# The end of a backward chain: the last block's turned keys in another buffer, and four of its stores at the end of the order

## The chip, the cores and the metric

The kernel runs on one core of one Trainium2 chip. The metric is the device time of one execution in microseconds. The kernel before takes 2858.67 us, the median of three runs (2856.47 to 2862.91).

## The reference, cut to what matters

The forward pass is a sum of three terms: the input, a recurrent attention over segments of 32 rows with 8 memory rows that each segment hands to the next, and a two-layer feed-forward branch with a squared ReLU. The reference returns its output and the gradients of all ten inputs and weights.

```python
for s in range(n_seg):                      # 64 segments
    xs = x[:, s * seg_len:(s + 1) * seg_len, :].copy()
    h = jnp.concatenate([mem, xs], axis=1)  # 8 memory rows + 32 rows
    q = jnp.einsum('btd,dhe->bhte', h, Wq)  # k, v in the same way
    ...
    o = jnp.einsum('bhte,hed->btd', o, Wo)
    mem = o[:, :M, :].copy()
...
return x + _A_ref(xn, ...) + _B_ref(xn, ...)
...
_out, _vjp = jax.vjp(_f, A_x, A_mem0, A_Wq, A_Wk, A_Wv, A_Wo, B_w1, B_b1, B_w2, B_b2)
```

Because each segment's memory rows come from the segment before, the backward pass must go through the 64 segments one after the other, from the last to the first. The gradients of the four attention weights are products over all 2048 rows and all 512 memory rows ("left" rows in the code), and can be made once the chain is through.

## The kernel before, in words

The kernel has five stages: the feed-forward branch, the forward chain over 64 segments, a pass over the left rows, the backward chain over 64 segments, and the products that give the weight gradients. The change concerns the end of the backward chain and the beginning of the products.

*The backward chain.* Four segments make a block; there are 16 blocks, taken from block 15 down to block 0, so that "the last block" is block 0. A block has 128 ordinary rows and 32 left rows. The order of work is written by hand: `B_ORDER` (line 1158) is four strings of operation names, one for each segment of a block, and `play` (line 652) goes through them and calls the operations. Each `+` behind a name lets it run one place earlier: for a segment's operation one segment, for a block's operation (`L.` ahead of the name) one block. An operation that a block does not have under that name is skipped. On each queue the chain's instructions keep this order; loads of the next stage can stand between them.

The operations of block 0 that matter here, in the order in which `play` calls them, with the operations of the last segment in between:

- `vo0`, `vo1`, `ko0`, `qo0`, `ko1`, `qo1` (`so`, line 1245) store the block's value, key and query gradients from the tiles `gv`, `gk`, `gq` (`G4`, line 1191) to `S_GB` in DRAM, 512 KB each, on SP's queue. In the other blocks they are called `Vo0`, `Ko0` and so on and stand at other places of the strings.
- `qst` of block 1, called between `qo0` and `ko1` of block 0: the store of block 1's turned left queries from the buffer `gNat` to `S_GL`.
- `G`, `H`, `I` with a number (line 1260): products of the left rows with the weights on TensorE, into PSUM tiles `ps_RL`, summed by VectorE (line 1267).
- `ktr`, `vtr`, `qtr` (`nt`, line 1278): the left keys, values and queries are turned. For all blocks but block 0 a DMA transpose does it. For block 0 it is done by eight TensorE transposes into two PSUM tiles `ps_tr`, copied to SBUF by ScalarE and VectorE (lines 419 and 422).
- `kst`, `vst`, `qst` (line 1292): the turned rows are stored to `S_GL` on SP's queue.
- `gs` (line 1233): four transposes of the gradient rows into `ps_gm` and a copy; `sx` stores `S_XG`, `sl` stores `S_XGL`.

The turned rows of blocks 15 to 1 all lie in one buffer with the tag `gNat`, one after the other. Block 0's keys take the same buffer; its values and queries take the buffers of `gON` and `gOT`, which the last segment no longer needs. The tile `qN` (line 1343) holds the query rows of a segment for the backward products `kp0` and `kp1` (line 623); it is in the pool `be` and has one buffer. `ps_RL`, `ps_tr`, `ps_gm` and the chain's other single PSUM tiles share four banks, which go round.

*The products* (line 1506 on). Sixteen products come one after the other, each with 20 steps of accumulation over row groups `rc`, in the order 1 to 19 and then 0. The first takes its columns from `S_ON` and `S_OL` (tile `gn`) and its rows from `S_GM` and the gradient (tiles `GOc`). It works on eight output tiles in eight PSUM banks at once, so that each step has eight matmuls (line 1653). The second has the same rows and other columns, with four output tiles at a time. The key and query gradients in `S_GB` are read by the last eight products.

The tiles of this stage lie where those of the chain were; each load waits until the old tiles under it are free. Loads of the first three products are issued on GpSimd's queue in this order: quarters of `gn` alternating with groups of `GOc` (row groups 1 to 3, 4 to 7, 8 to 11, 12 to 15), four loads of the last group of `GOc`, four of `gn`'s left rows from `S_OL`, and then the second product's, of which one quarter goes on SP's queue. The group 0 of `GOc` goes on ScalarE's queue.

Of the kernel before, what the change touches and what calls it, by code (L numbers as in the profile page):

```python
# [10 lines left out]
BF16 = mybir.dt.bfloat16  # L11
F32 = mybir.dt.float32
P = 128
# [13 lines left out]
def kernel(  # L27
# [35 lines left out]
    L = M + SEG  # L63
# [39 lines left out]
    KH = H // HG  # L103
# [61 lines left out]
    def transpose_to(ps_ap, in_ap, base=0):  # L165
        k = in_ap.shape[0]
        nc.tensor.transpose(ps_ap, in_ap, ident[base:base + k, base:base + k])
# [42 lines left out]
    with sb("p1b", 2) as p1b, sb("p1", 1) as p1:  # L210
# [90 lines left out]
        for rb in range(NRB):  # L301
# [38 lines left out]
            xb = xq[rb]  # L340
# [77 lines left out]
    def acp(out, in_):  # L418
        nc.scalar.copy(out, in_)  # L419
# [15 lines left out]
    def turned_heads(W):  # L435

        return lambda h: W[:, :, h * P:(h + 1) * P]
# [263 lines left out]
    with psum("fr", 4) as fr, psum("fpp", 1) as fpp, \  # L701
# [5 lines left out]
        def tr(name):  # L707
            return fr.tile([P, 4 * P], BF16, name=name, tag="r")
# [11 lines left out]
        def block(b):  # L720

            if b not in blk:
                shapes = {"kL": (fs, [P, KH, HG, NL], BF16), "OT": (fs, [P, HG, KH, SPB, SEG], BF16),
                          "X": (fs, [P, DC, P], BF16),
                          "kM": (fo, [P, KH, HG, NL], BF16), "vTM": (fo, [P, KH, HG, NL], BF16),
                          "XT": (fs, [P, DC, SPB, SEG], F32), "qL": (fo, [P, KH, HG, NL], BF16),
                          "VL": (fs, [P, GW], BF16), "vM": (fo, [P, GW], BF16), "EL": (fo, [P, KH, KW], BF16),
                          "OTL": (fo, [P, KH, HG, NL], BF16),
                          "bb": (fo, [P, D], BF16)}

                def make(n):
                    if n == "X" and b == 0:
                        return X0
                    pool, shape, dt = shapes[n]
                    return pool.tile(shape, dt, name=n, tag=n)
                blk[b] = Tiles(make)
            return blk[b]
# [256 lines left out]
    with sb("la", 2) as la, sb("ls", 2) as ls, sb("lo", 1) as lo_, sb("wg", 2) as wg, psum("lpp", 1) as lpp, psum("lr", 4) as lr:  # L994
# [148 lines left out]
        with tc.manual_schedule():  # L1143
# [4 lines left out]
            for b in range(NB + 1):  # L1148
                for nm in LB_ORDER:
                    k = nm.rstrip("-")  # L1150
# [18 lines left out]
        "kg1+++++ qg1+++++ ra+++++ klb1+++++ L.H3+ ta+++++ rb+++++ tb+++++ Ha+++++ Hb+++++ xb+++++ o0mm++++++ L.ra3+ "  # L1169
# [20 lines left out]
    with sb("bq", 1) as bq, sb("bt", 1) as bt, sb("bs", 2) as bs, sb("be", 1) as be, psum("bpp", 1) as bpp, psum("br", 4) as br:  # L1190
# [30 lines left out]
        def left(b):  # L1221
            B_ = block(b)
            ps, st, o = {}, {}, {}
            src = {"v": "gvL", "k": "gkL", "q": "gqL"}
            o["lq"] = lambda: dma(B_["gqL"][:], S_GQL[b])

            def following(f):

                return lambda: f(b - 1) if b > 0 else None
            for n, f in loads.items():  # L1230
                o[n] = following(f)

            def gs():
                if b > 0:
                    nc.sync.dma_start_transpose(B_["GN"][:], gts[b][:].rearrange("p c r -> p (c r)"))
                else:
                    ps["gm"] = tr("ps_gm")
                    for c in range(DC):
                        transpose_to(ps["gm"][:, c * P:(c + 1) * P], gts[b][:, c, :])
                    acp(B_["GN"][:], ps["gm"][:].rearrange("p (c d) -> p c d", c=DC))  # L1240
            o["gs"] = gs
            o["gst"] = lambda: (dma if b > 0 else nc.scalar.dma_start)(S_GM[b], B_["GN"][:].rearrange("p c d -> p (c d)"))
            for t, n in enumerate("qkv"):
                for x in range(2):
                    def so(n=n, t=t, gs=slice(2 * x, 2 * x + 2) if n == "v" else slice(0, HG),
                           ks=slice(0, KH) if n == "v" else HALF[x]):
                        dma(S_GB[b, t][:, gs, ks], G4[n][:, gs, ks].rearrange("p g k j r -> p g k (j r)"))
                    o["%so%d" % (n.upper() if b > 0 else n, x)] = so

            jobs = [(turned_heads(Wqkv[t]), src[n], k) for t, n in ((2, "v"), (1, "k"), (0, "q")) for k in range(KH)]  # L1250
            for i in range(4):
                for x, nm in enumerate("GHI"):
                    def G_(i=i, x=x):
                        if ("R", i) not in ps:
                            ps["R", i] = big("ps_RL")
                            ps["n", i] = 0
                        ps["n", i] += 1
                        for m, (W, n, k) in enumerate(jobs[6 * i + 2 * x:6 * i + 2 * x + 2]):
                            for g in range(HG):
                                nc.tensor.matmul(ps["R", i][32 * g:32 * g + 32, :].rearrange("p (a b) -> p a b", b=P),  # L1260
                                                 lhsT=B_[n][:, k, g, :], rhs=W(g * KH + k), start=(ps["n", i] == 1 and m == 0),
                                                 stop=(ps["n", i] == 3 and m == 1), tile_position=(0, 32 * g))
                    o["%s%d" % (nm, i)] = G_
                if i == 0:
                    o["ra0"] = lambda: ENGS["L.ra0"](B_["R4"][:], ps["R", 0][:])
                else:
                    o["ra%d" % i] = lambda i=i: nc.vector.tensor_tensor(out=B_["R4"][:], in0=ps["R", i][:],
                                                                        in1=B_["R4"][:], op=ALU.add)
            turn_ops(o, big, lambda: B_["R4"], st)

            def xt():
                st["XL"] = bt.tile([P, DC, SPB, M], F32, name="b_XL", tag="XL" if b > 0 else "gST0")
                left_sums(st["XL"], st["T"])
            o["xt"] = xt
            o["sl"] = lambda: dma(S_XGL[b], st["XL"][:])

            for t, n in enumerate("qkv"):
                def nt(n=n):

                    tag = "gNat" if b > 0 else {"k": "gNat", "v": "gON", "q": "gOT"}[n]  # L1280
                    st[n] = bt.tile([P, KH, P], BF16, name="gNat", tag=tag)
                    if b > 0:
                        nc.sync.dma_start_transpose(st[n][:], B_[src[n]][:].rearrange("p k g r -> p k (g r)"))
                    else:
                        for p in range(2):
                            pt = tr("ps_tr")
                            for k in range(4):
                                transpose_to(pt[:, k * P:(k + 1) * P],
                                             B_[src[n]][:, 4 * p + k].rearrange("p g r -> p (g r)"))
                            (acp, vcp)[p](st[n][:, HALF[p], :], pt[:].rearrange("p (k e) -> p k e", k=4))  # L1290
                o[n + "tr"] = nt
                o[n + "st"] = lambda n=n, t=t: dma(S_GL[b].rearrange("g r t c -> (g r) t c")[:, t, :],
                                                   st[n][:].rearrange("p k e -> p (k e)"))

            o["sx"] = lambda: dma(S_XG[b], B_["XT"][:].rearrange("p c j r -> p c (j r)"))
            return o
# [209 lines left out]
    with sb("p5a", 1) as p5a, sb("p5h", 1) as p5h, sb("p5", 2) as p5, sb("p5g", 1) as p5g, \  # L1506
# [120 lines left out]
        for i, (t, g) in enumerate(COLS):  # L1627
# [16 lines left out]
            for x, js in enumerate(jobs[k:k + each] for k in range(0, len(jobs), each)):  # L1644
                if x in ((), (), (2, 6), (2, 6))[i] if i < 4 else x == 4:
                    b = todo.pop(0)
# [48 lines left out]
```

## Time and profile before

| | us |
|---|---|
| median of the runs | 2858.67 (2856.47 to 2862.91) |
| the profiled execution, its own time | 2865.94 |
| span of that execution, first to last instruction | 2864.2 |
| TensorE matmuls busy | 2648.7 |
| VectorE busy | 1297.5 |
| ScalarE busy | 976.9 |
| GpSimd busy | 660.1 |

The last 563 us of the span, from 2301 on, belong to the products; the end of the backward chain lies in the 40 us ahead of that. A timeline row gives the start in us from the beginning of the span, the duration, the engine (PE is TensorE, ACT ScalarE, DVE VectorE, POOL GpSimd, SPq what SP's queue issues), the line, the operation, what it writes and reads, the number of instructions put together, and in brackets the idle time ahead of it with what ended it. "issue" there means that the profile shows nothing that the engine waited for.

### The profile page before, as it was taken

How to read it: one execution, taken by the hardware profiler on the slowest of the kernel's cores; microseconds unless marked ns; L12 is line 12 of the kernel's file. 1: busy time of each engine (PE TensorE's matmuls, PEld its weight loads, DVE VectorE, ACT ScalarE, POOL GpSimd, SP SyncE). 2: the span in 40 equal slices, each digit the busy share in tenths (PEclk: the TensorE clock that was granted, in tenths of full speed). 3: DMA queues.
4: the chain of work that ended last, by engine and by line, in shares of the span. 5: the costliest groups of instructions: out<-in, count | busy, mean ns of one | idle time of the engine just before them, and what ended most of it. 6: DMA issues, size and time to landing. Idle time of an engine off the chain costs nothing. (4 is left out here: it accounts for less than half of the span.)

```text
span 2864.2 us, 116882 instructions
## 1 busy us (share of the span) xinstructions
PE 2648.7 (92%) x52315; PEld 1448.9 (51%) x52405; DVE 1297.5 (45%) x3819; ACT 976.9 (34%) x2266; POOL 660.1 (23%) x1280
## 2 busy tenths in 40 slices
PE   7998999999999997888998898899898799999999
PEld 3444555555555555456554555555555344444444
DVE  4544666666666665344555555555554401100000
ACT  2323544444444445232333333333333211111111
POOL 1000000000000000223433334343443333322221
PEclk9999999999999999999999999999999999999999
DMA  9765589899989899988677877787777799999992
GB/s 255 263 198 177 159 198 225 202 217 226 211 201 221 215 213 190 279 237 219 151 180 196 203 176 177 182 215 186 176 186 205 227 298 222 203 204 207 208 218 63
DMA packets 840440, 586.76 MB, mean 205 GB/s; under 512 B 638001, under 2 KB 727746, under 8 KB 836610
## 3 DMA queue, kind: packets, MB, share of 16 engines
q1 hardware_dynamic: 798722, 455.76, 70.1%
q0 software_dynamic: 40928, 123.25, 14.5%
q8 instruction: 411, 6.73, 1.0%
q14 instruction: 91, 0.75, 0.1%
q10 hardware_dynamic: 288, 0.26, 0.0%
HBM read 184.95 MB, written 248.79 MB: 151 GB/s over the span
## 5 line engine op out<-in xcount | busy, mean ns | idle before, releaser
L1653 PE MATMUL ps_gw<-gn,HNc 128*128 128x512 bf16 x1884 | 414.6, 379 | 1.9
L1653 PEld LDWEIGHTS <-HNc 128*128 128x128 bf16 x1920 | 187.9, 98 | 223.8
L419 ACT CAST f_N<-ps_proj 128x512 bf16<-128x512 f32 x320 | 184.0, 581 | 197.4 <-PE ps_proj L374 194.1
L1583 ACT CAST wt<-ps_gw 128x512 bf16<-128x512 f32 x128 | 73.7, 589 | 440.6 <-PE ps_gw L1653 389.7
L374 PEld LDWEIGHTS <-X 128*32 128x32 bf16 x5760 | 144.5, 96 | 138.0 <-DVE X L537 20.6
L1566 DVE TENSOR_TENSOR gx<-ps_rows,gb 128x512 f32<-128x512 f32 x16 | 11.1, 692 | 423.0 <-PE ps_rows L1564 423.0
L884 POOL COPY kM<-f_kT 128x256 bf16<-128x256 bf16 x64 | 25.8, 403 | 752.5 <-DVE f_kT L422 567.1
L492 PE MATMUL ps_gR<-Wv,gv 128*32 128x512 bf16 x2048 | 136.7, 390 | 6.5 <-issue 4.5
L1653 PE MATMUL ps_gw<-GOc,gn 128*128 128x512 bf16 x626 | 138.4, 379 | 1.9 <-DVE gm L1499 1.1
L492 PE MATMUL ps_R<-Wo,OT 128*32 128x256 bf16 x4096 | 129.7, 277 | 9.3 <-DMA Wo<-in_A_Wo_dram 4.1
L492 PE MATMUL ps_gR<-Wk,gk 128*32 128x512 bf16 (+1 forms) x2048 | 128.6, 372 | 5.1 <-issue 5.1
L374 PE MATMUL ps_proj<-Wq,X 128*32 128x512 bf16 x1920 | 128.3, 384 | 2.1 <-issue 1.9
L1584 POOL DMA_DIRECT2D out_dram<-wt x120 | 65.0, 544 | 281.1 <-ACT wt L1583 274.3
L374 PE MATMUL ps_proj<-Wo,GT 128*32 128x512 bf16 x2048 | 123.9, 384 | 5.3 <-DVE GT L1305 4.9
L419 ACT CAST gON<-ps_proj 128x512 bf16<-128x512 f32 x128 | 75.0, 586 | 155.5 <-PE ps_proj L374 155.5
L492 PE MATMUL ps_gR<-Wq,gq 128*32 128x512 bf16 (+1 forms) x2048 | 119.5, 350 | 8.3 <-issue 8.2
L374 PE MATMUL ps_proj<-Wk,X 128*32 128x512 bf16 x1920 | 125.0, 384 | 0.9 <-issue 0.2
L374 PE MATMUL ps_proj<-Wv,X 128*32 128x512 bf16 x1920 | 122.0, 378 | 0.0
L1341 POOL COPY PD<-b_P 32x320 bf16<-32x320 bf16 x256 | 115.3, 450 | 16.7 <-DMA b_P<-S_A 4.9
L492 PEld LDWEIGHTS <-OT 128*32 128x32 bf16 x4096 | 105.0, 98 | 18.0 <-issue 11.9
L419 ACT CAST gk<-b_pp 128x256 bf16<-128x256 f32 x128 | 48.1, 376 | 171.0 <-PE b_pp L623 168.0
L492 PEld LDWEIGHTS <-gq 128*32 128x32 bf16 x2816 | 75.1, 98 | 56.4 <-issue 20.5
(291 smaller groups left out, 5269.2 us busy)
## 6 DMA issues: line engine op xcount, KB each, us to landing
S_A<-f_N SPq DMA_DIRECT2D x64, 512.0 KB
out_dram<-wt POOLq DMA_DIRECT2D x134, 128.0 KB, 5.4
S_A<-f_N SPq DMA_DIRECT2D x64, 256.0 KB
S_GB<-gv SPq DMA_DIRECT2D x32, 512.0 KB
S_GB<-gk SPq DMA_DIRECT2D x32, 512.0 KB
S_GB<-gq SPq DMA_DIRECT2D x32, 512.0 KB
b_qN<-S_A POOLq DMA_DIRECT2D x63, 256.0 KB, 3.9
b_kN<-S_A POOLq DMA_DIRECT2D x63, 256.0 KB, 5.1
```

The source lines that it names most:

```text
L374: nc.tensor.matmul(o, lhsT=hT[:, dc, :], rhs=x, start=(dc == 0), stop=(dc == DC - 1), tile_position=(0, 32 * g))
L419: nc.scalar.copy(out, in_)
L492: nc.tensor.matmul(R[32 * g:32 * g + 32, 0:(cs.stop - cs.start) * P].rearrange("p (a b) -> p a b", b=P), lhsT=XT(k, g), rhs=x[:, cs, :], s ...
L884: o["km"] = lambda: nc.gpsimd.tensor_copy(B_["kM"][:, :, :, lc], T["kT"][:, :, :, M:2 * M])
L1341: nc.gpsimd.tensor_copy(PD[32 * g:32 * g + 32, g], C["P"][32 * g:32 * g + 32, :, KW - L:KW])
L1566: nc.vector.tensor_tensor(out=gx[:], in0=ps[:], in1=gb[:], op=ALU.add)
L1583: nc.scalar.copy(wt[:], ps[:])
L1584: eng(dst, wt[:])
L1653: nc.tensor.matmul(ps[:], lhsT=l(rc), rhs=r(rc), start=(n == 0), stop=(n == RC_ALL - 1))
```

## The change

Two things are changed, both for block 0 alone. Its turned keys are put into a tile of the pool `be` with the tag `qN`, so into the buffer of the query rows, where they had the tag `gNat` in the pool `bt`. And `ko0`, `ko1`, `qo0`, `qo1` are taken out of the third string and put behind `L.sl` in the second, without a `+`; for block 0 this is the end of everything that `play` calls. Four names of segment operations go from the end of the second string to the beginning of the third with one `+` less, which is the same place. All other operations keep their order.

```diff
-        "vg1+++++ kea0+++++ d41+++++ klb0+++++ L.sl tu1+++++ keb0+++++ kg0+++++ qp1+++++ L.qtr+ qea0+++++ ldp++++++ "
+        "vg1+++++ kea0+++++ d41+++++ klb0+++++ L.sl L.ko0 L.ko1 L.qo0 L.qo1 tu1+++++ keb0+++++ kg0+++++ qp1+++++ "
...
-        "keb0+++++ L.ko0++ pb+++++ kg0+++++ d41+++++ kp1+++++ tu1+++++ qeb0+++++ qea0+++++ L.qo0++ klb0+++++ L.qst+ "
-        "qp1+++++ kla0+++++ kla1+++++ L.ldk++ kea1+++++ keb1+++++ L.ko1++ qeb1+++++ L.G0++ L.xt+ qg0+++++ L.I0++ "
-        "kg1+++++ L.Vo1++ klb1+++++ qea1+++++ L.qo1++ qg1+++++ L.G2++ ra+++++ rb+++++ ta+++++ tb+++++ Ha+++++ "
+        "d31+++++ L.ldv++ vg1+++++ kea0+++++ keb0+++++ pb+++++ kg0+++++ d41+++++ kp1+++++ tu1+++++ qeb0+++++ "
+        "qea0+++++ klb0+++++ L.qst+ qp1+++++ kla0+++++ kla1+++++ L.ldk++ kea1+++++ keb1+++++ qeb1+++++ L.G0++ L.xt+ "
+        "qg0+++++ L.I0++ kg1+++++ L.Vo1++ klb1+++++ qea1+++++ qg1+++++ L.G2++ ra+++++ rb+++++ ta+++++ tb+++++ "
...
-                    tag = "gNat" if b > 0 else {"k": "gNat", "v": "gON", "q": "gOT"}[n]
-                    st[n] = bt.tile([P, KH, P], BF16, name="gNat", tag=tag)
+                    tag = "gNat" if b > 0 else {"k": "qN", "v": "gON", "q": "gOT"}[n]
+                    st[n] = (be if tag == "qN" else bt).tile([P, KH, P], BF16, name="gNat", tag=tag)
```

More of the change, by code (lines that the diff above doesn't have):

```diff
@@ L1166 @@
         "L.G3+ L.I3+ s1+++++ kp0+++++ qp0+++++ d11+++++ vea+++++ d21+++++ vg0+++++ vlb+++++ d31+++++ veb+++++ "
[2 rows of a table removed]
-        "kg1+++++ qg1+++++ ra+++++ klb1+++++ L.H3+ ta+++++ rb+++++ tb+++++ Ha+++++ Hb+++++ xb+++++ o0mm++++++ L.ra3+ "
[8 rows of a table removed]
[11 rows of a table added]
         "o0fl++++++ o1ev++++++ vp0++++++ o0te++++++ xb+++++ L.Qo1++ ldk0+++++ o1fl++++++ ldp+++++++ s0++++++ "
```

13 rows, old and new, of the table B_ORDER are left out of this document.

## Prediction

> **What bounds the kernel now.** I read the page first, then the table by stretches around the end of the backward chain, then the table of waits there, then the timelines of TensorE, SP and GpSimd in those stretches. The page:
>
> ```profile
> span 2864.2 us, 116882 instructions
> PE 2648.7 (92%) x52315; PEld 1448.9 (51%) x52405; DVE 1297.5 (45%) x3819; ACT 976.9 (34%) x2266; POOL 660.1 (23%) x1280
> PE ps_gw L1653 19%; PE ps_rows L1564 0%; DVE gm L1499 0%; ACT wt L1583 0%; ACTq L1583 0%
> L1653 PE MATMUL ps_gw<-gn,HNc 128*128 128x512 bf16 x1884 | 414.6, 379 | 1.9
> ```
>
> TensorE is busy for 92% of the span, and the chain that ended last is the final stage of weight-gradient products (L1653), with 1.9 us of idle time before 1884 of its matmuls. So nothing inside that stage is to be had, and whatever lets it start earlier shortens the whole kernel, as long as its loads keep up. The table by stretches (columns: stretch, length, then busy time and count of PE, PEld, DVE, ACT, POOL, then granted clock, DMA share, GB/s) shows where it starts:
>
> ```profile
> 2275.00:2290.00 15.00, 5.22 (x96) 2.73 (x89) 1.40 (x5) 1.18 (x2) 2.85 (x6) 0.82 1.05 385
> 2290.00:2301.00 11.00, 6.88 (x69) 3.57 (x70) 4.63 (x11) 2.35 (x4) 5.21 (x8) 0.78 0.97 339
> 2301.00:2336.00 35.00, 34.79 (x159) 15.80 (x162) 0.00 (x0) 2.02 (x5) 5.63 (x10) 1.00 0.86 265
> ```
>
> From 2301 on TensorE is full; in the 15 us from 2275 it works 5.22 us while the DMA engines are full at 385 GB/s. The waits there (total, times, longest), then TensorE's own rows:
>
> ```profile
> ACT gNat L419 <- DMA S_GL<-gNat: 11.7, 1, 11.7
> PE ps_gm L167 <- ACT gNat L419: 11.0, 1, 11.0
> ```
>
> ```profile
> 2271.31 0.18 PE L623 MATMUL b_pp<-gST,b_kNL 8*128 8x32 bf16 x1 [4.20 <-issue]
> ...
> 2279.06 0.62 PE L167 MATMUL ps_tr<-ident,b_gkL 128*128 128x128 bf16 x8
> 2279.61 0.61 PE L1260 MATMUL ps_RL<-Wk,b_gkL 128*32 128x512 bf16 x8
> 2291.24 0.59 PE L167 MATMUL ps_gm<-ident,GT 128*128 128x128 bf16 x4 [11.02 <-ACT gNat L419]
> 2291.76 1.04 PE L1260 MATMUL ps_RL<-Wk,b_gkL 128*32 128x512 bf16 x8
> 2292.59 1.07 PE L1260 MATMUL ps_RL<-Wq,b_gqL 128*32 128x512 bf16 x8
> 2293.59 1.03 PE L167 MATMUL ps_tr<-ident,b_gvL 128*128 128x128 bf16 x8
> 2294.93 1.05 PE L1260 MATMUL ps_RL<-Wq,b_gqL 128*32 128x512 bf16 x16 [0.30 <-ACT gNat L419]
> ```
>
> The eight transposes at 2279.06 turn the left keys of the last block (operation `ktr`). Their copy out of PSUM, into `gNat`, waits for a store out of that same buffer: `qst` of the block before, `S_GL<-gNat`. Four PSUM banks go round in this stage; all four are taken, so the next transposes (`ps_gm`) wait for the copy: 11.02 us, on the only path to the last stage. SP's queue shows why the store was late:
>
> ```profile
> 2262.85 0.87 SPq L1247 DMA_DIRECT2D S_GB<-gv  x2
> 2265.29 0.56 SPq L1247 DMA_DIRECT2D S_GB<-gk  x1
> 2265.95 0.80 SPq L1247 DMA_DIRECT2D S_GB<-gq  x1
> 2266.79 5.45 SPq L1292 DMA_DIRECT2D S_GL<-gNat  x1
> 2272.35 1.49 SPq L1247 DMA_DIRECT2D S_GB<-gk  x1
> 2273.93 5.88 SPq L1247 DMA_DIRECT2D S_GB<-gq  x1
> 2279.90 5.72 SPq L1295 DMA_DIRECT2D S_XG<-b_XT  x1
> ```
>
> It stood behind four stores of 512 KB each on its queue, beside the loads of the last stage on GpSimd's queue:
>
> ```profile
> q0 software_dynamic: 1196, 4.19, 73.1%
> q1 hardware_dynamic: 1446, 1.56, 30.5%
> ```
>
> These two rows (packets, MB, share) are for 2275 to 2290: SP's queue (q1) moved 1.56 MB, 104 GB/s, while GpSimd's (q0) moved 4.19 MB.
>
> **The change, part by part.** (1) *The buffer.* For the last block `ktr` writes into the tile of `qN` instead of `gNat`. The copy then waits for the last reader of `qN` instead of the store:
>
> ```profile
> L623 PE MATMUL b_pp<-gS,b_qN x32: 174/174/188, 2264.0 to 2266.6; 32*128 32x40 bf16 x32
> 2290.61 0.59 ACT L419 COPY gNat<-ps_tr 128x512 bf16<-128x512 bf16 x1 [11.71 <-DMA S_GL<-gNat]
> ```
>
> That reader starts last at 2266.6, on the engine that later does the transposes, so it is over. ScalarE's copy takes 0.59 us and can begin when the first four of the eight transposes are done, at about 2279.4; it ends near 2280.0, before TensorE ends the group in front of `ps_gm` (2279.61 + 0.61 = 2280.22). The whole 11.02 us goes. The value and query halves of the last block (`vtr`, `qtr`) use other tiles already and show no DMA wait. No instruction is added.
>
> (2) *The clock behind the wait.* Eight matmuls of 128x512 take 0.61 us before the wait and 1.04 and 1.07 after it; eight transposes 0.62 and 1.03; the granted clock of the two stretches is 0.82 and 0.78 against 1.00 later. Without the wait the three groups give back 0.43 + 0.46 + 0.41 = 1.30 us. Bounds: nothing, if the copies of ScalarE and VectorE between them set the pace, and 1.3; I take 1.3, since the wait that TensorE has inside this piece is 0.3 us. [...]
>
> (3) *The four moved stores* (`ko0`, `ko1`, `qo0`, `qo1`) leave SP's queue between 2265 and 2280 and are issued behind all other stores of the chain. Four issues of 0.56 + 0.80 + 1.49 + 5.88 us go with them; SP is not on the path. Nothing reads these 2.1 MB until the key and query products, hundreds of microseconds later. `qst` comes out from behind them, but after (1) nobody on the path waits for it. What they cost is DMA time later: 2.1 MB at 385 GB/s are 5.4 us, beside the loads of the second product. Either none of it shows or all 5.4; I take none, for the cover named below.
>
> (4) *A wait that the change adds.* The last stage puts its tiles over the old ones. GpSimd's rows:
>
> ```profile
> 2267.56 0.75 POOL L1598 DMA_DIRECT2D GOc<-S_GM  x1 [0.83 <-PE b_pp L623]
> 2271.79 0.56 POOL L1602 DMA_DIRECT2D GOc<-in_grad_out_dram  x1 [3.48 <-PE b_pp L623]
> ...
> 2293.11 1.52 POOL L1527 DMA_DIRECT2D gn<-S_ON  x2 [5.27 <-PE ps_RL L1260]
> ...
> 2303.29 0.76 POOL L1527 DMA_DIRECT2D gn<-S_ON  x1 [3.46 <-DMA gn<-S_ON]
> ```
>
> The load at 2267.56 (blocks 12 to 15 of `GOc`) waited 0.83 us for the matmuls that read `qN`: by the program's allocation it lies on `qN` (its 4 KB begin 1,984 bytes ahead of it). Now it must wait until the turned keys are stored from there (`kst`). Behind it on GpSimd's queue stand four loads of `GOc`, four of `S_OL` and all of the second product's. When does `kst` land? Issued at about 2280.4. Bounds: 2.1 us, an unloaded store of this kind, by the rows
>
> ```profile
> 2249.96 0.32 SPq L1292 DMA_DIRECT2D S_GL<-gNat  x1
> ...
> 2252.08 1.25 SPq L1283 DMA_TRANSPOSE gNat<-b_gqL  x1
> ```
>
> where the refill of the same buffer starts at 2252.08; and 23.8 us, the late `qst` (2266.79 to 2290.61). Its queue now holds only `S_XG` ahead of it: 0.52 MB with its own, at 104 GB/s 5.0 us, so 2285.4. The load of `GOc` itself:
>
> ```profile
> DMA to landing us min/median/max: 10.9/15.6/19.4
> ```
>
> for the `GOc` loads of this stretch, so it lands at 2304.8 at the latest. It is needed in the twelfth of 20 steps of the first product, each eight matmuls: 35.0 us over 159 matmuls are 0.22 us each, 88 of them 19.4 us after the start. The start is
>
> ```profile
> 2300.71 11.60 PE L1653 MATMUL ps_gw<-GOc,gn 128*128 128x512 bf16 x51 [1.12 <-DVE gm L1499]
> ```
>
> less 12.3, or 2288.4, and the need 2307.8. Cover: 3.0 us at the slow end, 11.5 at the fast. The second product is needed 160 matmuls after the start, at 2323.6. Its first load left at 2293.11 and was in by 2303.29 (the row there waits for it). It may now go at 2285.4 + 0.75 + 8 x 0.56 = 2290.6, and even with 4.2 MB pushed in front of it (the four stores, and the loads behind the gate, as many bytes again; 10.9 us at 385 GB/s) it is in by 2311.7, with 11.9 us to spare.
>
> **Sum:** 11.0 + 1.3 = 12.3 us. The span goes from 2864.2 to 2851.9, the profiled execution from 2865.94 to 2853.6. That execution was 7.3 us above the median of the runs, 2858.67; taking the gain from the median gives **2846.4 us**. About 0.2% (5.7 us) is what a measurement of this kernel can tell from no change.
>
> **The rivals.**
> *A, the DMA engines take part of it back.* They are full from 2275 on; a start 12.3 us earlier meets the same bytes. For it: share 1.05 and 0.97 in the table. Against: the cover of 11.9 us. Price, if none of the moved bytes is hidden: 5.4 us, so 2858.67 - 12.3 + 5.4 = 2851.8. [...]
>
> *B, slower: the gate on GpSimd's queue.* If `kst` lands as late as `qst` did (23.8 us, at 2304.2) and the load takes 19.4, it is in at 2323.6, 15.8 us after its need, and the kernel is 3.5 us slower than before: 2862.2. It decides from the point where landing plus load pass 2307.8 + 12.3 = 2320.1. Against: the four stores that held `qst` up are no longer ahead.
>
> *C, the change doesn't do what it says:* the banks stay taken for another reason, such as the next store or copy at the same place, and the time stays at 2858.7. Against: the waits name this DMA alone.
>
> *D, more than forecast.* TensorE stood 4.20 us at 2271.31 for nothing that the profile shows, in full DMA traffic, ahead of the spot. With a shorter SP queue it may go too: 2858.67 - 12.3 - 4.2 = 2842.2. I expect it to stay, since GpSimd's loads and the two `gv` stores ahead of it stay.
>
> **How the numbers follow.** Forecast 0.62 (its own range 2844 to 2850), A 0.13, B 0.11, C 0.08, D 0.06. The range reaches from just under D to just over A, 2841 to 2854; that holds the forecast, A and D, 0.81. Faster by over 0.2% (below 2853.0) are forecast and D and nearly all of A: 0.80; within 0.2% C and the rest of A: 0.09; slower B: 0.11.
>
> **What would show it.** In the changed kernel ScalarE's copy of the keys should start near 2279.5 without a DMA wait, `ps_gm` at about 2280.3, the groups behind it take about 0.61 us, L1653 start near 2288.4 and keep its 1.9 us of idle time, and GpSimd's load at 2267.6 move to about 2285 with `S_GL` as its releaser. The forecast is wrong if L1653 shows idle time at its 89th or 161st matmul, if TensorE waits at `ps_gm` for something new, or if `kst` lands after 2290.

## The result, and the profile after

The changed kernel takes 2850.53 us, the median of 15 runs (2839.97 to 2861.89), against 2862.40 us for the kernel before in as many runs. The ratio is 0.9961 with a 95% interval of 0.9943 to 0.9979, so it is faster by 11.2 us, between 6.0 and 16.3. Single executions of one kernel lie up to 34 us apart (2838.82 to 2873.19 for the kernel before), and what follows is therefore read from stretches of the traces, not from whole spans. The page and the table by stretches of the changed kernel, its own execution taking 2851.62 us:

```profile
span 2849.8 us, 116970 instructions
PE 2660.2 (93%) x52405; PEld 1452.3 (51%) x52405; DVE 1296.4 (45%) x3819; ACT 976.6 (34%) x2266; POOL 659.3 (23%) x1280
```

```profile
2275.00:2290.00 15.00, 11.91 (x113) 5.51 (x106) 4.63 (x11) 2.68 (x5) 5.99 (x11) 0.89 1.00 339
2290.00:2301.00 11.00, 11.00 (x53) 4.98 (x51) 0.00 (x0) 0.00 (x0) 5.04 (x8) 1.00 1.05 375
```

TensorE, which worked 5.22 of the 15 us from 2275 on, now works 11.91 of them, and from 2290 on it is already full with the products. Its timeline:

```profile
2275.49 0.62 PE L167 MATMUL ps_tr<-ident,b_gkL 128*128 128x128 bf16 x8
2276.04 0.61 PE L1260 MATMUL ps_RL<-Wk,b_gkL 128*32 128x512 bf16 x8
2276.59 0.40 PE L167 MATMUL ps_gm<-ident,GT 128*128 128x128 bf16 x4
2276.92 0.61 PE L1260 MATMUL ps_RL<-Wk,b_gkL 128*32 128x512 bf16 x8
2277.36 0.61 PE L1260 MATMUL ps_RL<-Wq,b_gqL 128*32 128x512 bf16 x8
2277.90 0.62 PE L167 MATMUL ps_tr<-ident,b_gvL 128*128 128x128 bf16 x8
2279.02 1.05 PE L1260 MATMUL ps_RL<-Wq,b_gqL 128*32 128x512 bf16 x16 [0.51 <-ACT gNat L419]
...
2282.62 0.63 PE L545 MATMUL ps_sum<-identF,b_R 128*128 128x128 f32 x4 [1.46 <-DVE b_R L1267]
...
2284.81 15.56 PE L1653 MATMUL ps_gw<-GOc,gn 128*128 128x512 bf16 x64 [1.12 <-DVE gm L1499]
```

ScalarE's copy of the turned keys waits for the transposes alone:

```profile
2275.93 0.59 ACT L419 COPY gNat<-ps_tr 128x512 bf16<-128x512 bf16 x1 [0.59 <-PE ps_tr L167]
```

The bracket with 11.02 us at `ps_gm` is gone, and the groups behind it take 0.61 and 0.62 us where they took 1.04, 1.07 and 1.03. From the first key transposes to the first matmul of the products it is now 2284.81 - 2275.49 = 9.32 us. Before it was 2300.71 - 2279.06 = 21.65 us. I call this **the stretch**; it is 12.33 us shorter. SP's queue and GpSimd's in the changed kernel:

```profile
2259.65 0.86 SPq L1247 DMA_DIRECT2D S_GB<-gv  x2
2260.56 0.59 SPq L1292 DMA_DIRECT2D S_GL<-gNat  x1
...
2276.65 0.32 SPq L1292 DMA_DIRECT2D S_GL<-gNat  x1
...
2284.57 1.50 SPq L1247 DMA_DIRECT2D S_GB<-gk  x2
2286.11 5.58 SPq L1247 DMA_DIRECT2D S_GB<-gq  x2
```

```profile
2257.70 1.51 POOL L1527 DMA_DIRECT2D gn<-S_ON  x2 [4.68 <-PE ps_proj L374]
...
2281.39 0.75 POOL L1598 DMA_DIRECT2D GOc<-S_GM  x1 [17.87 <-DVE gNat L422]
```

The key and query stores come last, the old `qst` stands right behind `gv`, and GpSimd stands 17.87 us in front of the fourth `GOc` load. The profile names VectorE's copy into `gNat` as its releaser, but that copy was over at 2276.57; the load waited on for the store of the turned keys, issued at 2276.65.

The spans differ by 14.4 us, more than the stretch. GpSimd's first load of the products leaves at 2257.70 here and left at 2260.90 before, ahead of everything that was changed: 3.2 us of the difference lie there and belong to the execution. In the other direction, the products take 565.0 us here (2284.81 to 2849.8) and took 563.5 before (2300.71 to 2864.2). Their first 5 us, in the changed kernel and then before:

```profile
2284.81:2289.81 5.00, 5.00 (x16) 1.92 (x16) 0.00 (x0) 0.00 (x0) 2.38 (x5) 0.68 1.06 329
```

```profile
2300.71:2305.71 5.00, 4.94 (x23) 2.28 (x24) 0.00 (x0) 0.00 (x0) 0.76 (x1) 1.00 1.04 409
```

The granted clock there is 0.68 instead of 1.00, and 16 matmuls go through instead of 23. The seven that are missing are worth 7 x 0.22 = 1.5 us. No other idle time shows in the products (count, then busy time and mean ns of one, then idle time):

```profile
L1653 PE MATMUL ps_gw<-gn,HNc 128*128 128x512 bf16 x1920 | 416.5, 379 | 0.0
L1653 PE MATMUL ps_gw<-GOc,gn 128*128 128x512 bf16 x640 | 140.7, 382 | 1.2 <-DVE gm L1499 1.1
```

### The profile page after: what moved, and what is told of

Read it like the earlier page. It is cut to its first block, busy times and chain, and to the rows that moved or that the text cites. A ratio compares the mean times of both kernels' runs of the same rounds, so it can differ in the third digit from the quotient of the medians.

```text
span 2849.8 us, 116970 instructions
## 1 busy us (share of the span) xinstructions
PE 2660.2 (93%) x52405; PEld 1452.3 (51%) x52405; DVE 1296.4 (45%) x3819; ACT 976.6 (34%) x2266; POOL 659.3 (23%) x1280
## 3 DMA queue, kind: packets, MB, share of 16 engines
q8 instruction: 411, 6.73, 1.0%
## 4 chain that ended last, share of the span: by engine, by line
PE 85%; issue 4%; DMA 4%; DVE 4%; SPq 2%; ACT 2%; POOL 0%; ACTq 0%; DVEq 0%; POOLq 0%
PE ps_gw L1653 19%; PE ps_proj L374 16%; PE ps_gR L492 12%; PE ps_R L492 5%; PE ps_RL L1260 3%; PE ps_tr L167 3%; PE b_pp L623 3%; PE ps_L L374 3%; PE ps_sc L464 2%; PE f_pp L623 2%; PE ps_B L345 2%; PE b_T L528 2%; PE ps_gxb L354 2%; PE f_T L528 2%; PE ps_w L1106 2%
## 5 line engine op out<-in xcount | busy, mean ns | idle before, releaser
L1653 PE MATMUL ps_gw<-gn,HNc 128*128 128x512 bf16 x1920 | 416.5, 379 | 0.0
L1653 PEld LDWEIGHTS <-HNc 128*128 128x128 bf16 x1920 | 187.9, 98 | 223.9
L1653 PE MATMUL ps_gw<-GOc,gn 128*128 128x512 bf16 x640 | 140.7, 382 | 1.2 <-DVE gm L1499 1.1
```

The costliest lines, as they stand in the source:

```text
L1653: nc.tensor.matmul(ps[:], lhsT=l(rc), rhs=r(rc), start=(n == 0), stop=(n == RC_ALL - 1))
```

## The experiments

My theory was that the wait came from the place of `qst` on SP's queue, behind the two `gv` stores, `ko0` and `qo0`; any edit that takes it from there, or takes the keys out of its buffer, should then bring the stretch to the same 9.3 us. Against it stood the traffic as a whole, and the need for both edits together. Each ratio is to the kernel before, run beside it.

**Each edit alone.** In the first run the keys go into `qN` and the order is as before. In the second the order is as in the changed kernel and the keys stay in `gNat`.

```diff
-                    tag = "gNat" if b > 0 else {"k": "gNat", "v": "gON", "q": "gOT"}[n]
+                    tag = "gNat" if b > 0 else {"k": "qN", "v": "gON", "q": "gOT"}[n]
```

> The buffer of the keys is changed, the four stores stay where they were. The measure in all these runs is the stretch from the first of the eight key transposes to the first matmul of L1653: 21.65 us before (2279.06 to 2300.71), 9.32 us in the changed kernel (2275.49 to 2284.81). My theory (the wait was the place of qst on SP's queue, and either edit alone takes it away): stretch about 9.3 us. The keys' store now lands behind the four stores, about 14 us after the key transposes, so GpSimd's gate on the fourth GOc load opens at about 14 instead of 6 us, and L1653 has 0 to 4 us of idle time at its 89th matmul; time 8 to 12 us below the kernel before. Rival 1 (the full DMA engines cost the time, whatever buffer): L1653 loses most of the 11 us again by waiting for loads, time within 3 us of before. Rival 2 (only both edits together help): stretch above 15 us.

> The four stores are moved to the end, the keys stay in gNat. My theory: qst has only the two gv stores ahead of it and lands about 14 us after its issue, before the key transposes; stretch 9.3 to 10 us, no wait of the copy for a DMA above 1 us, the fourth GOc load not gated (issued right behind the third), time as the changed kernel within 2 us. Rival 2 (the buffer is what counts): the copy still waits 5 us or more for S_GL, stretch 14 to 22 us.

TensorE and GpSimd with the buffer alone:

```profile
2270.68 0.62 PE L167 MATMUL ps_tr<-ident,b_gkL 128*128 128x128 bf16 x8
...
2280.00 0.58 PE L1653 MATMUL ps_gw<-GOc,gn 128*128 128x512 bf16 x1 [1.12 <-DVE gm L1499]
```

```profile
2282.57 0.75 POOL L1598 DMA_DIRECT2D GOc<-S_GM  x1 [23.91 <-DMA out_dram<-gm]
```

And with the stores alone:

```profile
2272.46 0.62 PE L167 MATMUL ps_tr<-ident,b_gkL 128*128 128x128 bf16 x8
...
2281.78 4.91 PE L1653 MATMUL ps_gw<-GOc,gn 128*128 128x512 bf16 x21 [1.12 <-DVE gm L1499]
```

```profile
2259.53 0.75 POOL L1598 DMA_DIRECT2D GOc<-S_GM  x1 [0.72 <-PE b_pp L623]
```

The stretch is 9.32 us in both. The ratios are 0.9950 (0.9925 to 0.9975) and 0.9974 (0.9953 to 0.9994). Either edit alone does the whole work, and rival 2 is out. With the buffer alone the keys' store stands behind `ko0`, `ko1`, `qo0` and `qo1`, and the gate on GpSimd's queue opens 11.9 us after the key transposes, where it opens at 5.9 in the changed kernel. TensorE has no wait at the 89th matmul all the same. With the stores alone there is no gate: the load leaves at 2259.53, released by the last readers of `qN`.

**One store moved, the traffic left.** `qst` of block 1 goes ahead of `ko0` and `qo0`, which it stood behind; the two `gv` stores stay ahead of it. Its counterpart puts it behind `ko1` and `qo1` too, so that six stores stand ahead of it. The strings serve all blocks, so `qst` of the earlier blocks changes its place with it; the other operations keep theirs.

```diff
-        "keb0+++++ L.ko0++ pb+++++ ... L.qo0++ klb0+++++ L.qst+ "
+        "keb0+++++ L.qst+ L.ko0++ pb+++++ ... L.qo0++ klb0+++++ "
```

> The kernel before with one store moved alone: qst of block 1 goes ahead of ko0, qo0, ko1, qo1 on SP's queue; keys in gNat, the four stores and their traffic where they were. My theory: qst lands before the key transposes; stretch 9.3 to 11 us, time 9 to 13 us below before. Rival 1 (traffic, not order): the DMA engines are as full as before, so the copy waits 5 us or more, stretch above 14 us.

> The kernel before with qst of block 1 moved back behind ko1 and qo1, so that three megabytes of stores stand ahead of it on SP's queue where before there are two (and one in the run with qst first). My theory (place on the queue): the wait grows by the time that SP's queue takes for one megabyte there, 1.05 MB at 104 GB/s, 10 us; stretch 28 to 34 us, ScalarE's copy waits 18 to 24 us, time 6 to 13 us above the kernel before. Rival 1 (the traffic as a whole ends at the same time, whatever the order): stretch 21 to 25 us, time within 4 us of before.

SP's queue and TensorE with `qst` first:

```profile
2253.99 0.90 SPq L1247 DMA_DIRECT2D S_GB<-gv  x2
2254.93 0.51 SPq L1292 DMA_DIRECT2D S_GL<-gNat  x1
```

```profile
2270.78 0.62 PE L167 MATMUL ps_tr<-ident,b_gkL 128*128 128x128 bf16 x8
...
2280.10 0.52 PE L1653 MATMUL ps_gw<-GOc,gn 128*128 128x512 bf16 x1 [1.12 <-DVE gm L1499]
```

With `qst` last, TensorE:

```profile
2286.57 0.62 PE L167 MATMUL ps_tr<-ident,b_gkL 128*128 128x128 bf16 x8
...
2303.90 0.59 PE L167 MATMUL ps_gm<-ident,GT 128*128 128x128 bf16 x4 [16.17 <-ACT gNat L419]
...
2314.11 1.24 PE L1653 MATMUL ps_gw<-GOc,gn 128*128 128x512 bf16 x4 [1.12 <-DMA gn<-S_ON]
```

With `qst` first, the stretch is 9.32 us and the ratio 0.9959 (0.9939 to 0.9979): the stores and their bytes stay, and the gain is all there, so rival 1 is out. With `qst` last, the wait is 16.17 us instead of 11.02, the stretch 27.54 us and the ratio 1.0042 (1.0016 to 1.0068). That ratio means 12 us (4.6 to 19.4), of which the stretch holds 5.9; where the rest lies is open, and the interval allows for none. So it is the place on the queue: two, four and six stores ahead of `qst` give no wait, 11 and 16 us, on one and the same traffic. The size was missed, though. I expected 10 us for another megabyte at 104 GB/s and measured 5.2. The rate was carried over into a time in which less was left of GpSimd's loads: in the run with `qst` last, SP's queue moved 0.87 MB from 2286 to 2296 (87 GB/s), beside 2.89 MB on GpSimd's, and 1.34 MB from 2296 to 2303.3 (184 GB/s), beside 0.68.

**The gate on GpSimd's queue.** The changed kernel with the keys in two other buffers of the same size: that of `qNL`, under which no early tile of the products lies, and that of `vl`, which lies under the first `GOc` load.

```diff
-                    tag = "gNat" if b > 0 else {"k": "qN", "v": "gON", "q": "gOT"}[n]
-                    st[n] = (be if tag == "qN" else bt).tile([P, KH, P], BF16, name="gNat", tag=tag)
+                    tag = "gNat" if b > 0 else {"k": "qNL", "v": "gON", "q": "gOT"}[n]
+                    st[n] = (be if tag == "qNL" else bt).tile([P, KH, P], BF16, name="gNat", tag=tag)
```

> The changed kernel with the keys in the buffer of qNL instead of qN: no early tile of the products lies there, so GpSimd's fourth GOc load is not gated. My theory (the gate is covered by about 10 us): stretch 9.3 us, the fourth GOc load issued right behind the third, time as the changed kernel within 2 us. Rival (the gate costs something that is not seen as a wait): 3 us or more below the changed kernel.

> The changed kernel with the keys in the buffer of vl, which lies under the first GOc load (row groups 1 to 3) instead of the fourth. It prices the gate on GpSimd's queue. My theory: GpSimd stops at its third load until the keys' store has landed, about 6 us after the key transposes; five of the first product's loads (4.6 MB with the left rows) then come within 12 to 15 us of one another, and L1653 needs them from 9.3 us on: its first matmul comes 10 to 15 us after the key transposes and it shows 1 to 8 us of idle time later in the first two products; time 1 to 10 us above the changed kernel. Rival (the gate costs nothing wherever it lies): stretch 9.3 us, no idle time in L1653.

GpSimd and TensorE with the free buffer, and then TensorE with the early gate:

```profile
2276.74 0.75 POOL L1598 DMA_DIRECT2D GOc<-S_GM  x1 [0.72 <-PE b_pp L623]
```

```profile
2287.75 0.62 PE L167 MATMUL ps_tr<-ident,b_gkL 128*128 128x128 bf16 x8
...
2297.08 0.59 PE L1653 MATMUL ps_gw<-GOc,gn 128*128 128x512 bf16 x1 [1.12 <-DVE gm L1499]
```

```profile
2261.10 0.62 PE L167 MATMUL ps_tr<-ident,b_gkL 128*128 128x128 bf16 x8
...
2271.76 0.59 PE L1653 MATMUL ps_gw<-GOc,gn 128*128 128x512 bf16 x1 [2.47 <-DMA GOc<-S_GM]
```

Without a gate the stretch is 9.33 us and the ratio 0.9971 (0.9947 to 0.9996), not to be told from the changed kernel's: the gate costs nothing where the change put it. With the gate at the first `GOc` load the products wait for that load, 2.47 us instead of 1.12, and the stretch is 10.66 us (2271.76 - 2261.10). The ratio, 0.9981 (0.9957 to 1.0004), cannot be told from the others. So the gate costs 1.35 us of wait under the load that is needed first, and none that shows under the fourth. I had expected more idle time further on in the products; there was none beyond this wait. But the clock at their start fell further than in the changed kernel, to 0.50:

```profile
2271.76:2276.76 5.00, 4.78 (x11) 1.77 (x13) 0.00 (x0) 0.00 (x0) 1.04 (x2) 0.50 1.05 413
```

Eleven matmuls go through in these 5 us instead of 16, and the products take 566.2 us (2271.76 to 2838.0) instead of 565.0. With the wait the early gate costs some 2.6 us in the trace, which is too little to show in the ratio.

**The 4 us ahead of the stretch.** TensorE stands 3.6 to 4.6 us at a matmul on `b_kNL`, with no releaser in the profile, in every kernel so far. For the next run the first product's column tiles change places, so that GpSimd's first load has to wait for the `gv` stores. My guess was that instructions for TensorE are fetched late there.

```diff
-                return [p5a.tile([P, 4, CW], BF16, name="gn5", tag="gn%d" % q) for q in range(RC_ALL // 4)]
+                t_ = {q: p5a.tile([P, 4, CW], BF16, name="gn5", tag="gn%d" % q) for q in (1, 2, 3, 4, 0)}
+                return [t_[q] for q in range(RC_ALL // 4)]
```

> The changed kernel with the first product's column tiles in other places: the first quarter lies on gv, so that GpSimd's first load of the products waits until the two gv stores have landed, about 5 us later than now. It asks about the 3.7 to 4.6 us that TensorE stands 8 us ahead of the key transposes with no releaser in the profile (matmul on b_kNL, L623). My theory: the instruction queue's fetch (16 KB for 256 instructions of TensorE) is late there because the products' loads fill the DMA engines; with the loads held back the idle time there falls below 1 us, the groups behind it run at full clock, and L1653 still starts without waiting for its loads: time 3 to 6 us below the changed kernel. Rival (the time belongs to something else, such as the matmul's own operands or the gv stores): the idle time stays at 3 us or more, time as the changed kernel or, if loads come too late, above it.

TensorE in the changed kernel, and then with the loads held:

```profile
2267.57 0.18 PE L623 MATMUL b_pp<-gST,b_kNL 8*128 8x32 bf16 x1 [3.67 <-issue]
2267.68 1.05 PE L1260 MATMUL ps_RL<-Wv,b_gvL 128*32 128x512 bf16 x8
```

```profile
2266.00 0.17 PE L623 MATMUL b_pp<-gST,b_kNL 8*128 8x32 bf16 x1 [2.00 <-issue]
2266.10 0.61 PE L1260 MATMUL ps_RL<-Wv,b_gvL 128*32 128x512 bf16 x8
```

GpSimd's first load in this run:

```profile
2264.86 1.51 POOL L1528 DMA_DIRECT2D gn<-S_ON  x2 [11.76 <-DMA S_GB<-gv]
```

The queue that the profile calls "instruction" (packets, MB, share), in the changed kernel between 2265.0 and 2265.5, and with the loads held between 2263.5 and 2264.0:

```profile
q8 instruction: 1, 0.02, 11.1%
```

```profile
q8 instruction: 1, 0.02, 11.0%
```

Over the whole span of the changed kernel this queue has 411 packets and 6.73 MB, 16.4 KB each; shared out among them, TensorE's 104,810 matmuls and weight loads are 255 to a packet (an estimate that takes all of them for TensorE's). In each of the eleven traces one packet of this queue starts 2.2 to 2.4 us before TensorE goes on, whatever the length of the standstill. In the changed kernel it starts 1.3 us after the standstill began, and with the loads held 0.3 us before, although the matmuls ahead begin within 0.1 us of each other (2263.26 and 2263.35). The held loads let it come earlier, and the standstill falls to 2.00 us. It did not fall below 1 us, as I had expected, because the 2.2 to 2.4 us from the packet to the next matmul stay. From the matmuls ahead to the key transposes it is 8.94 us (2263.35 to 2272.29) against 12.23 (2263.26 to 2275.49), 3.3 us less: 1.7 of them are the shorter standstill, and the group of eight matmuls behind it takes 0.61 us where it took 1.05. The stretch is 9.32 us, and the ratio to the kernel before 0.9932 (0.9909 to 0.9955). That the loads make the standstill longer is shown: it was 2.00 and 2.64 us in the two runs that hold them, and 3.64 to 4.56 in the nine others. That TensorE waits for the instructions in this packet is argued from the fixed distance; no run changes the packet alone.

**The clock at the start of the products.** The changed kernel with ten matmuls more, whose output nobody reads, in the two waits of 1.46 and 1.12 us, to see whether the clock still falls with the waits filled; and the same with the loads held.

```diff
+            for i in range(5):
+                nc.tensor.matmul(x[:], lhsT=ident[:], rhs=G4["k"][:, 0, 0:4].rearrange("p k j r -> p (k j r)"), start=True, stop=True)
```

> The changed kernel with ten more matmuls of 128x512 that nobody reads: five where TensorE waits 1.46 us for VectorE's sums, five where it waits 1.12 us for the end of the chain. It asks why the products start at half clock: granted clock 0.66 to 0.70 in the first 5 us of L1653 in the changed kernel and the runs with the buffer alone, with qst first, with the free buffer and with the loads held, 1.00 before, with the stores alone and with qst last. [...]

> The changed kernel with the products' loads held until gv is stored, as in the run with held loads, and with the ten filling matmuls. A second look at the clock, and the version that the runs so far point to. My theory: idle time on b_kNL about 2 us, stretch 9.3 to 9.6 us, clock 1.00 at the start of L1653, products 563.5 us; time 0 to 3 us below the run with held loads and 3 to 7 us below the changed kernel (ratio to before 0.992 to 0.995). Rival (the fillers cost what they save): clock 1.00 but stretch 10.5 us or more, time as with held loads.

The first 5 us of the products in the first of the two, and TensorE ahead of them:

```profile
2288.61:2293.61 5.00, 5.00 (x24) 2.28 (x25) 0.00 (x0) 0.00 (x0) 1.02 (x2) 1.00 1.06 315
```

```profile
2284.91 1.25 PE L1305 MATMUL ps_fill<-gk,ident 128*128 128x512 bf16 x5
2286.35 0.66 PE L545 MATMUL ps_sum<-identF,b_R 128*128 128x128 f32 x4 [0.18 <-DVE b_R L1267]
```

In the run with the stores alone, which has the same waits and no fillers, the first 5 us were:

```profile
2281.78:2286.78 5.00, 4.95 (x23) 2.27 (x24) 0.00 (x0) 0.00 (x0) 2.91 (x6) 1.00 1.05 300
```

With the fillers the clock is 1.00 and 24 matmuls go through; so it is in the second run, and the products take 563.5 us in both. The stretch keeps its 9.31 us. In the times this does not show: 2853.87 us in one execution, and a ratio of 0.9952 (0.9927 to 0.9976) for the second, where I expected it below the run with held loads alone. Its standstill on `b_kNL` was 2.64 us. The best ratio measured is that of the held loads without fillers, whose interval overlaps with that of the changed kernel.

## Why the prediction was right

- *The total.* The forecast was 2846.4 us and the range 2841 to 2854; 2850.53 lies in the range, but 4.1 us above the forecast, just outside its own 2844 to 2850 and nearer to rival A's 2851.8. Of the 4.1 us, 3.7 are the kernel before, whose median over 15 runs is 2862.40 us where three runs had given 2858.67. As a gain it is 12.3 us forecast and 11.2 measured (6.0 to 16.3). This interval also holds rival A's 12.3 - 5.4 = 6.9 us, so the total alone does not decide between the two; the traces do.
- *The wait.* 11.02 us at `ps_gm` were to go and went; ScalarE and VectorE copied the keys without a DMA wait, and `ps_gm` started 1.10 us after the key transposes (forecast: 2280.3 - 2279.06 = 1.2).
- *The clock behind it.* 1.30 us were taken; the stretch fell by 12.33, so 1.3 came back at that place (granted clock 0.50 from 2291.20 to 2294.50 before, 1.00 from 2275 to 2282 now). What the prediction did not see is that the clock then fell later: in the traced execution of the changed kernel the products begin at 0.68 and lose 1.5 us. It did not fall in the run with the stores alone, so this term comes and goes between the runs. The sum in the trace is 12.3 - 1.5 = 10.8 us, and the forecast of 12.3 was too high by this term; the measured 11.2 us cannot tell the two apart.
- *The moved stores.* They were costed at nothing, and no load of the second product came late: 0.0 and 1.2 us of idle time in the products, 1.1 of it ahead of their first matmul. With the fillers, and the stores still moved, the products take 563.5 us, as before the change. Rival A did not show.
- *The gate.* It was forecast at 6.3 us after the key transposes (2285.4 against 2279.06) and opened at 5.9; even at 11.9 us, with the buffer alone, it cost nothing. Rival B's mechanism is there, but its point of decision was far off.
- *Rival C* fell with the waits. *Rival D*: 4.20 us before, 3.67 after, so it stayed, as forecast. Its length depends on GpSimd's loads: 2.00 and 2.64 us in the runs that hold them, 3.64 to 4.56 in the others.
- Of the two edits the prediction took the buffer as the one that removes the wait and the moved stores as costing nothing. The runs show that they are two cures for one ailment, and that moving one store ahead of two others is a third. Of the four stores ahead of `qst` the change moves two, `ko0` and `qo0`; the `gv` stores stay, and `qst` was early enough behind them.
- The 1.9 us of idle time in L1653 before belong to matmul records that the trace lacks (1884 of 1920); with all of them, as in the changed kernel, it is 0.0.

## What to carry to other kernels

When a copy waits for a store out of its buffer, look at what stands ahead of that store on its queue before looking for another buffer: the order of the stores alone gave the same stretch of 9.32 us here. When a late tile is put into a reused buffer, look up which of the next stage's loads lies on it and when that load is needed; a wait in front of a load that is needed some 19 us into the products (the first 88 matmuls took 19.59 us before) was free, and one in front of the first load cost 1.35 us, and another 1.2 us by the clock behind it.

## What the runs showed of the hardware

TensorE's clock fell with no idle piece above 1.46 us in the 6.3 us ahead of the products. In the changed kernel pieces of 0.51, 1.46 and 1.12 us stand there; the granted clock was 0.97 from 2282.00 to 2284.81, 0.50 over the first 2 us of the products and 1.00 again from 2288.81 on. Over the first 5 us of the products it was 0.68 in the changed kernel, 0.70 with the buffer alone and with the free buffer, and 0.66 with `qst` first; with held loads it was 0.66 from 2281 to 2286, around the start at 2281.61. With the same idle pieces it was 1.00 in the run with the stores alone. It was 1.00 too in the kernel before and with `qst` last, where the first piece is 0.30 us and stands shortly behind the wait of 11.02 or 16.17 us; in the kernel before the clock was 0.50 from 2291.20, behind that wait, to 2294.50 and 1.00 from 2296.00 on. With 2.47 us in place of the 1.12 it was 0.50 (the early gate). With the two longer pieces filled it was 1.00 both times. That several short pieces add up is the author's reading of these runs, one trace each, and was not shown: no run fills one piece alone, none changes the short groups of f32 transposes between them (0.63 and 0.60 us), and what parts the run with the stores alone from the others is open.

TensorE's standstill ahead of the stretch ends 2.2 to 2.4 us after the start of a packet of the queue "instruction" in all eleven traces. A standstill of 2.00 us left the group of eight matmuls behind it at 0.61 us; one of 2.64 us (held loads with fillers) was followed by 1.04.
